# Retention followed by a two-layer MLP with a sine, on one core: the values' columns side by side in PSUM, stores in two pieces, seven products from block 1 on

## The chip, the cores and the metric

The kernel runs on one core of a Trainium2 chip. A core has TensorE (PE; its weight loads are listed as PEld), VectorE (DVE), ScalarE (ACT), GpSimd (POOL) and SyncE (SP), which here issues DMAs; all but SyncE compute. The metric is the device time of one execution in microseconds, median of several runs; lower is better.

## The reference

Eight batches with eight heads, 576 positions and head dimension 64 go through retention (attention without softmax, with a decay), and the result, 4608 rows of 512, through two matrices with h + sin²(alpha h)/alpha between them.

```python
scores = 1/sqrt(64) * np.matmul(q, k.transpose(0, 1, 3, 2))     # q, k, v: (8, 8, 576, 64)
gamma = 1.0 - 2.0 ** (-5.0 - np.arange(8))
Dmat = np.where(rel >= 0, gamma[:, None, None] ** rel, 0.0)      # rel = pos[:, None] - pos
x = np.matmul(scores * Dmat, v)       # then heads side by side: (4608, 512)
h = x @ w_in                          # (512, 2048)
s = np.sin(alpha * h)
g = h + s * s / (alpha + 1e-09)
out = g @ w_out                       # (2048, 512)
```

## The kernel before

**Blocks.** The first 512 positions of each batch are a block, 0 to 7; the last 64 positions of all eight batches form block 8. In a block, positions are taken in chunks of 128 rows: inside a chunk scores are computed and masked, and what came before enters through a state per head.

**One block, step by step.** LD loads 256 positions of q, k or v; partition i holds the two rows 2i and 2i + 1 of a chunk side by side. (k and v of blocks 5 to 7 are loaded with the chunk's two halves of 64 rows instead; `HALVED = 5`.) CA casts to f16 and multiplies in the decay. TU turns q and k on PE, and TK evicts that (blocks 0 and 1); later blocks use a DMA transpose, XP. OU multiplies k and v into the chunks' sums, EV or TS evicts them, and MA, MB and ST make the states from them. SC are the scores, MK the mask. VA and VB multiply masked scores with v: VA for the products whose rows and bank belong to different halves of PE's rows, VB for those of the same half, and between them stands RL, an empty instruction that waits for VA. SA adds the state's part into the same PSUM columns. KP evicts the result to x. Then, for each of 16 units of w_in, PR is the product with w_in, SI the sine, SQ its square and PD the sum g.

**Where the values' columns stand.** VA, VB and SA write 128 columns for a chunk, two groups of 64: rows 2i (r = 0) and rows 2i + 1 (r = 1). The group r goes to every second column, in the rows' own order (lines 574 and 607).

**The product with w_out.** Blocks 0 and 1 do it in the plain way: G2, four units of w_out at a time, for each of four chunks, evicted by FI and stored by OS. From block 2 on it is done with seven products of quarters in place of eight (Strassen in Winograd's form): TT makes differences of w_out's quarters once, SM four sums of g's quarters for each block, each in two pieces, PP the seven products of 8 units and two chunks each, CP copies four of them out of PSUM, AD adds three more, and OQ stores a quarter of the block's output. SM, CP and AD can be given to different engines.

**What sets the order.** The whole program is a list of steps, `STEPS`, written out by a planner. A step's name holds its kind and indices; after a colon stands its engine (A, V, G for ACT, DVE, POOL), and `name=number` places a buffer. Each engine runs its own steps in the list's order and waits by semaphores for what a step reads and writes. All stores and all loads of q, k, v, as well as the DMA transposes, go through SyncE's queue in that order; the loads of w_in (WI, four column groups of 512, units 4g to 4g + 3) and w_out (WO) go through GpSimd's. KB steps are dummy products of zeros on PE (128x256) that keep it at work while it has nothing else in the first blocks.

**Stores.** A partition holds one row of a chunk, so an OS or OQ of blocks 0 to 7 is one DMA of 128 partitions. Block 8's two pieces are two DMAs of 64 partitions, since its rows come from two batches.

Of the kernel before, what the change touches and what calls it, by code (L numbers as in the profile page):

```python
# [23 lines left out]
CN; AR; EY; MC; Z0; ZE; FS; LD.0.q.0 raw.0.q.0=0; LD.0.k.0 raw.0.k.0=1; KB.25.256.6; LE.0.q rs.0.q=0  # L24
LD.0.q.1 raw.0.q.1=2; CA.0.q.0.0:V q16.0.0=1; TU.0.q.0.0 tr.0.q.0=0; LD.0.k.1 raw.0.k.1=3; AT al=1; KB.28.256.6
CA.0.k.0.0:V k16.0.0=2; CA.0.k.0.1:G; LD.0.v.0 raw.0.v.0=4; CA.0.q.0.1:G; CA.0.q.1.2:V q16.0.1=3; WI.2
LD.0.v.1 raw.0.v.1=5; TU.0.q.0.1; TU.0.k.0.0 tr.0.k.0=2; TU.0.k.0.1; KB.2.256.6; TK.0.k.0.0:A kT.0.0=4; TK.0.k.0.1:V
TU.0.q.1.2 tr.0.q.1=3; CA.0.k.1.2:G k16.0.1=5; TK.0.q.0.2:V qT.0.0=6; KB.4.256.2; SC.0.0.0 sc.0.0.0=4
SC.0.0.1 sc.0.0.1=6; KB.4.256.2; MK.0.0.0 ret.0.0.0=7; LD.1.q.1 raw.1.q.1=6; TU.0.k.1.2 tr.0.k.1=0
CA.0.v.0.2:G v16.0.0=8; KB.6.256.2; MK.0.0.1 ret.0.0.1=9; TK.0.k.1.2:A kT.0.1=10; OU.0.0 kv.0.0.0=2 kv.0.0.1=4  # L30
TK.0.q.1.2:V qT.0.1=11; VA.0.0 o.0.0=6; TS.0.0:A kvs.0=7; KB.2.256.0; TS.0.1:V; ST.0.0:G s16.0=12; SC.0.1.1 sc.0.1.1=2
RL.0.0:V; SC.0.1.0 sc.0.1.0=4; WI.0; SA.0.0; VB.0.0; MK.0.1.0 ret.0.1.0=13; KB.21.256.0; LD.1.q.0 raw.1.q.0=8
MA.0.1:G s32.0.1=14; MK.0.1.1 ret.0.1.1=15; MB.0.1:G; CA.0.v.1.2:A v16.0.1=16; WI.1; LD.1.k.0 raw.1.k.0=9
KP.0.0.0:V x.0=10; OU.0.1 kv.0.1.0=0 kv.0.1.1=2; MA.0.2:G s32.0.2=17; VA.0.1 o.0.1=4; TS.0.2:A; KB.3.256.3; ST.0.1:G
RL.0.1:A; KP.0.0.1:A; MB.0.2:V; VB.0.1; KB.7.256.3; ST.0.2:V; MA.0.3:G s32.0.3=18; TS.0.3:V; SA.0.1; AC:V
PR.0.9.0 hps.0.9=0; CA.1.q.1.2:G q16.1.1=19; MB.0.3:V; KP.0.1.0:A; PR.0.8.0 hps.0.8=1; KP.0.1.1:A; KB.2.256.7
PR.0.8.1; LD.1.v.0 raw.1.v.0=11; PR.0.11.2 hps.0.11=2; WI.3; TU.1.q.1.2 tr.1.q.1=3; WO.0; PR.0.1.2 hps.0.1=4
PR.0.3.2 hps.0.3=5; SI.0.1 s.0.1=0; CA.1.q.0.2:V q16.1.0=20; PR.0.2.0 hps.0.2=6; SQ.0.1:G ss.0.1=1; SI.0.3 s.0.3=2
PR.0.9.1; PR.0.2.1; SQ.0.3:A ss.0.3=3; AI; TU.1.q.0.2 tr.1.q.0=7; SI.0.8 s.0.8=4; TK.1.q.1.2:V qT.1.1=21
SI.0.2 s.0.2=5; PD.0.1 gT.0=0; PR.0.0.2 hps.0.0=3; SI.0.11 s.0.11=6; TK.1.q.0.0:V qT.1.0=22; PD.0.3  # L40
PR.0.7.2 hps.0.7=4; SI.0.0 s.0.0=7; SQ.0.11:G ss.0.11=8; TK.1.q.0.1:V; SI.0.9 s.0.9=9; PR.0.6.2 hps.0.6=5
SQ.0.0:V ss.0.0=10; LD.1.k.1 raw.1.k.1=12; SQ.0.2:V ss.0.2=11; PR.0.4.2 hps.0.4=7; SI.0.6 s.0.6=12; PD.0.2
SI.0.7 s.0.7=13; PD.0.11; PR.0.10.2 hps.0.10=6; SQ.0.8:A ss.0.8=14; SQ.0.7:G ss.0.7=15; SQ.0.6:A ss.0.6=2
PR.0.5.2 hps.0.5=2; SQ.0.9:A ss.0.9=0; WO.1; PD.0.7; SI.0.10 s.0.10=1; PD.0.9; CA.1.k.0.2:G k16.1.0=23
PR.0.14.2 hps.0.14=4; SI.0.4 s.0.4=3; PD.0.0; SQ.0.4:A ss.0.4=6; PR.0.13.2 hps.0.13=0; LD.1.v.1 raw.1.v.1=13
SQ.0.10:A ss.0.10=7; PD.0.4; PR.0.12.2 hps.0.12=3; WO.2; LD.2.k.1 raw.2.k.1=14; CA.1.v.0.2:A v16.1.0=24; PD.0.6; WO.3
PR.0.15.0 hps.0.15=7; PD.0.8; SI.0.13 s.0.13=5; G2.0.3.0 op.0.3=5; SI.0.5 s.0.5=11; SQ.0.13:V ss.0.13=8
TU.1.k.0.2 tr.1.k.0=1; SQ.0.5:A ss.0.5=4; PD.0.10; CA.1.k.1.2:G k16.1.1=25; PR.0.15.1; TK.1.k.0.2:A kT.1.0=26; PD.0.5
G2.0.1.0 op.0.1=6; PD.0.13; SI.0.12 s.0.12=12; OU.1.0 kv.1.0.0=1 kv.1.0.1=2; SI.0.14 s.0.14=13; TS.1.1:V kvs.1=15
TS.1.0:V; SQ.0.14:A ss.0.14=9; SC.1.0.1 sc.1.0.1=0; TT.1.1:G T1=1; PD.0.14; TU.1.k.1.2 tr.1.k.1=2; G2.0.3.1  # L50
TK.1.k.1.1:A kT.1.1=27; MK.1.0.1 ret.1.0.1=1; SQ.0.12:A ss.0.12=15; G2.0.0.0 op.0.0=4; TK.1.k.1.0:A; PD.0.12; TT.1.0:G
LD.2.v.1 raw.2.v.1=0; SI.0.15 s.0.15=0; SC.1.0.0 sc.1.0.0=0; SC.1.1.1 sc.1.1.1=2; MK.1.0.0 ret.1.0.0=3
SQ.0.15:A ss.0.15=10; G2.0.1.1; G2.0.3.2; PD.0.15; CA.1.v.1.0:A v16.1.1=4; CA.1.v.1.1:G; MA.1.1:G s32.1.1=2
MK.1.1.1 ret.1.1.1=10; OU.1.1 kv.1.1.0=7 kv.1.1.1=0; TS.1.3:A; SC.1.1.0 sc.1.1.0=0; MB.1.1:V; VA.1.0 o.1.0=2
TT.2.0:V T2=2; G2.0.1.2; MA.1.2:G s32.1.2=6; LD.2.q.0 raw.2.q.0=3; TS.1.2:V; MK.1.1.0 ret.1.1.0=7; G2.0.3.3; MB.1.2:G
# [175 lines left out]
def kernel(  # L231
# [10 lines left out]
    nc = tc.nc  # L242
# [4 lines left out]
    P = 128  # L247
# [686 lines left out]
```

## Time and profile before

| | |
|---|---|
| median of 3 runs | 316.77 us (316.67 to 316.96) |
| profiled execution, and its span | 316.97 us, 315.3 us |
| DMA | 49.88 MB, mean 158 GB/s |
| KB dummies on PE | 104 of 3609 matmuls |

The profile is of one execution. A group of instructions is listed with its line, engine, shapes, count, busy time, mean duration and the idle time ahead of it; the chain of waits is what the end hung on, followed backwards. In a list by time, the first figure is the start in us and the second the time that a merged row takes up. PE's matmuls overlap, so their busy time is larger than the distance from one to the next. A queue (SPq, POOLq) is the part of an engine that issues DMAs.

### The profile page before, as it was taken

What the parts mean: (1) busy time and instruction counts of PE and PEld (TensorE: products, weight loads), DVE (VectorE), ACT (ScalarE), POOL (GpSimd) and SP (SyncE); (2) the same over time, 40 slices, a digit from 0 to 9 for tenths busy, and PEclk for the clock granted to TensorE, in tenths of its full rate; (3) what the DMA queues carried; (4) which work ended last, traced back from release to release, by engine and by line L of the source; (5) the groups of instructions that cost most, each with busy time, mean ns of one, the idle gap of its engine ahead of it and who ended that gap; (6) DMA issues with size and microseconds to landing.
All of it is one profiled execution on the core that took longest, in us unless ns stands there. A gap on an engine that the chain in (4) does not pass through costs nothing.

```text
span 315.3 us, 8643 instructions
## 1 busy us (share of the span) xinstructions
PE 301.4 (96%) x3609; PEld 191.0 (61%) x3609; DVE 247.3 (78%) x354; ACT 184.2 (58%) x295; POOL 200.1 (63%) x174
## 2 busy tenths in 40 slices
PE   8979979999999999999999999999999999999993
PEld 5756444654454555666557657666666567555883
DVE  2656899499997899987778879797799986687732
ACT  1223974484736977858447857666167465678310
POOL 5656576555947857998969689753643534267830
PEclk9999999999999999999999999999999999999999
DMA  8999999459999899838898990626622000110047
GB/s 222 316 281 263 238 233 268 112 120 271 280 238 232 199 184 264 178 78 155 230 241 213 189 202 0 103 52 169 174 85 64 2 0 2 35 67 2 0 136 232
DMA packets 118454, 49.88 MB, mean 158 GB/s; under 512 B 69248, under 2 KB 117392, under 8 KB 118416
## 3 DMA queue, kind: packets, MB, share of 16 engines
q1 hardware_dynamic: 113984, 45.10, 58.8%
q0 software_dynamic: 4224, 4.19, 8.0%
q8 instruction: 28, 0.46, 0.6%
q14 instruction: 10, 0.08, 0.1%
q10 hardware_dynamic: 208, 0.04, 0.1%
HBM read 36.74 MB, written 9.44 MB: 146 GB/s over the span
## 4 chain that ended last, share of the span: by engine, by line
PE 71%; DVE 13%; ACT 4%; DMA 3%; issue 3%; SPq 3%; POOL 2%; POOLq 0%; DVEq 0%; ACTq 0%
PE banks L754 26%; PE banks L855 20%; PE banks L790 9%; PE banks L411 4%; PE banks L573 4%; DVE g L777 4%; PE banks L542 2%; DVE h L555 2%; DVE r L838 2%; PE banks L606 2%; DVE s L773 2%; PE banks L498 2%; ACT s L772 2%; SPq L420 1%; ACT s L762 1%
## 5 line engine op out<-in xcount | busy, mean ns | idle before, releaser
L754 PE MATMUL banks<-r,w_in 128*128 128x512 f16 (+1 forms) x608 | 138.6, 368 | 1.7 <-DVE g L777 1.3
L762 ACT ACTIVATE s<-banks,alpha 128x512 f16<-128x512 f32 x144 | 94.7, 686 | 56.3 <-PE banks L754 55.0
L777 DVE SCALAR_TENSOR_TENSOR g<-s,inva,banks 128x512 f16<-128x512 f16 x144 | 102.0, 741 | 19.9 <-ACT s L772 11.2
L754 PEld LDWEIGHTS <-w_in 128*128 128x128 f16 x608 | 57.4, 98 | 54.9 <-issue 4.4
L855 PEld LDWEIGHTS <-g 128*128 128x128 f16 x560 | 53.7, 98 | 14.8 <-issue 0.6
L773 POOL TENSOR_TENSOR s<-s 128x512 f16<-128x512 f16 x29 | 32.0, 1107 | 38.4 <-ACT s L762 38.4
L447 POOL TENSOR_TENSOR h<-r,cn 128x1024 f16<-128x1024 f32 (+1 forms) x24 | 44.4, 1864 | 5.3 <-DMA r<-in_k_dram 2.8
L772 ACT ACTIVATE s<-s 128x512 f16<-128x512 f16 x76 | 46.1, 628 | 1.2
L838 POOL TENSOR_TENSOR r<-g 128x1024 f16<-128x1024 f16 x15 | 32.5, 2171 | 20.2 <-DVE g L838 10.4
L855 PE MATMUL banks<-w_out,g 128*128 128x256 f16 x336 | 44.5, 273 | 0.0
L329 ACT COPY h<-banks 128x512 f32<-128x512 f32 (+2 forms) x30 | 18.4, 612 | 43.9 <-PE banks L855 23.7
L555 DVE TENSOR_TENSOR h<-banks,mask 128x1024 f16<-128x1024 f32 (+1 forms) x32 | 35.4, 1119 | 7.2 <-PE banks L542 6.3
L790 PE MATMUL banks<-w_out,g 128*128 128x512 f16 x128 | 30.5, 380 | 1.3 <-DVE g L777 1.3
L855 PE MATMUL banks<-r,g 128*128 128x256 f16 x224 | 29.7, 273 | 0.0
L773 DVE TENSOR_TENSOR s<-s 128x512 f16<-128x512 f16 x39 | 22.1, 585 | 7.6 <-ACT s L762 7.6
L855 PEld LDWEIGHTS <-r 128*128 128x128 f16 x224 | 21.7, 98 | 8.1 <-POOL r L838 0.8
L329 ACT CAST r<-banks 128x1024 f16<-128x1024 f32 (+1 forms) x22 | 17.5, 821 | 13.5 <-PE banks L606 9.0
L871 DVE TENSOR_TENSOR h<-banks,h 128x512 f32<-128x512 f32 x21 | 14.3, 687 | 8.7 <-PE banks L855 4.6
L790 PEld LDWEIGHTS <-g 128*128 128x128 f16 x128 | 11.7, 98 | 14.9 <-issue 2.3
L447 DVE TENSOR_TENSOR h<-r,cn 128x512 f16<-128x512 f32 (+1 forms) x16 | 15.4, 979 | 5.8 <-DMA r<-in_q_dram 4.6
L523 POOL TENSOR_TENSOR h<-r,cn 128x256 f32<-128x256 f32 x18 | 12.4, 690 | 10.5 <-DVE r L329 3.9
L573 PE MATMUL banks<-h 64*64 64x128 f16 (+1 forms) x512 | 18.5, 296 | 0.3 <-DVE h L555 0.3
(70 smaller groups left out, 300.3 us busy)
## 6 DMA issues: line engine op xcount, KB each, us to landing
r<-in_q_dram SPq DMA_DIRECT2D x16, 512.0 KB, 6.0
out_dram<-h SPq DMA_DIRECT2D x32, 256.0 KB, 2.8
r<-in_k_dram SPq DMA_DIRECT2D x10, 512.0 KB, 10.0
r<-in_v_dram SPq DMA_DIRECT2D x10, 512.0 KB, 6.7
r<-in_v_dram SPq DMA_DIRECT2D x24, 128.0 KB, 3.3
r<-in_k_dram SPq DMA_DIRECT2D x24, 128.0 KB, 3.7
w_in<-in_moe_w_in_dram POOLq DMA_DIRECT2D x4, 512.0 KB, 9.5
w_out<-in_moe_w_out_dram POOLq DMA_DIRECT2D x4, 512.0 KB, 10.8
```

The source lines that it names most:

```text
L329: return eng.copy(d_, s_) if eng is nc.scalar else eng.tensor_copy(d_, s_)
L447: return eng.tensor_tensor(dst[:, a0:a1].rearrange("p a r t d -> p t (a r) d"), t_.rearrange("p (t a) x -> p t a x", t=2)[:, :, a0:a1].rea ...
L555: return nc.vector.tensor_tensor(ret(b, p, y).rearrange("p t (z x) -> p (t z) x", z=2)[:, :, 0:n], bank(f"sc.{b}.{p}.{y}", 2).rearrange("p ...
L573: made.append(matmul(o[halves(e), t, c : c + 128].rearrange("p (i r) -> p r i", r=2)[:, :, i0:64], v16[halves(g), 4 * t + 2 * x + e, r, :] ...
L754: i = matmul(bank(hps)[:, cols], w_in16[:, a, u * P : (u + 1) * P], x_of(n)[:, a, cols], start=starts(hps), stop=(a == KT - 1), skip_group ...
L762: return nc.scalar.activation(small(f"s.{name}")[:, cols], bank(f"hps.{name}")[:, cols], mybir.ActivationFunctionType.Sin, bias=0.0, scale ...
L772: return nc.scalar.activation(ss_t, s_t, mybir.ActivationFunctionType.Square)
L773: return eng.tensor_tensor(ss_t, s_t, s_t, MULT)
L777: return nc.vector.scalar_tensor_tensor(g_of(n)[:, u, cols], small(f"ss.{name}")[:, cols], inva[:, u : u + 1], bank(f"hps.{name}")[:, cols ...
L790: i = matmul(bank(f"op.{n}.{c}"), g_of(n)[:, fk, c * P : (c + 1) * P], w_out16[:, fk, :], start=starts(f"op.{n}.{c}"), stop=True, skip_gro ...
L838: return eng.tensor_tensor(S[s], a, b, op)
L855: i = matmul(ps[:, 256 * c : 256 * c + 256], left[:, 0, 128 * c : 128 * c + 128], right[:, 0, :], start=starts(f"{BANK_OF[p]}.{n}"), stop= ...
```

## The change

It has four parts.

1. VA, VB and SA write the group r to 64 columns side by side: the first 64 of a chunk's 128 columns hold rows 2i, the next 64 rows 2i + 1. Everything after that has its rows in this order.
2. So a partition p of an output chunk holds row 2i + r with p = 64 r + i. OS and OQ store 64 partitions at a time, each to every second row; OQ does so for all blocks. Stores are now 72 DMAs where there were 40.
3. Block 1 uses the seven products as well: its G2, FI and OS steps (16, 4, 4) go, and 28 PP, 8 SM, 4 CP, 3 AD and 4 OQ come. Only block 0 is left with the plain product.
4. The list of steps is in a new order, with engines and buffers chosen anew: of the KB dummies 65 are left; the differences of w_out's quarters are all made while blocks 0 and 1 run.

```diff
 def values(b, p, same):
-    o[halves(e), t, c : c + 128].rearrange("p (i r) -> p r i", r=2)[:, :, i0:64],
+    o[halves(e), t, c : c + 128].rearrange("p (r i) -> p r i", r=2)[:, :, i0:64],
...
 def SA(b, p):
-    o[halves(e), t, c : c + 128].rearrange("p (i r) -> p r i", r=2),
+    o[halves(e), t, c : c + 128].rearrange("p (r i) -> p r i", r=2),
...
 def rows_of(n, c, m=1):
     if n == 8:
-        return out.rearrange("(b s) d -> b s d", s=S)[2 * c : 2 * c + 2 * m, 512:576, :]
-    return out[576 * n + 128 * c : 576 * n + 128 * (c + m), :]
+        return out.rearrange("(b s) d -> b s d", s=S)[2 * c : 2 * c + 2 * m, 512:576, :].rearrange(
+            "(c r) s d -> r s c d", r=2
+        )
+    r0 = 576 * n + 128 * c
+    return out[r0 : r0 + 128 * m, :].rearrange("(c i r) d -> r i c d", r=2, i=64)
...
 def OS(n, c):
-    x = rows_of(n, c)
-    return nc.sync.dma_start(x.rearrange("b s d -> (b s) d") if n == 8 else x, mid32(f"osb.{n}.{c}"))
+    nc.sync.dma_start(rows_of(n, c)[0, :, 0], mid32(f"osb.{n}.{c}")[halves(0)])
+    return nc.sync.dma_start(rows_of(n, c)[1, :, 0], mid32(f"osb.{n}.{c}")[halves(1)])
...
 def OQ(n, c):
-    if n < 8:
-        return nc.sync.dma_start(x.rearrange("(c p) d -> p c d", p=P), t)
-    x = x.rearrange("(c r) s d -> r s c d", r=2)
     nc.sync.dma_start(x[0], t[halves(0)])
     return nc.sync.dma_start(x[1], t[halves(1)])
...
-CN; AR; EY; MC; Z0; ZE; FS; LD.0.q.0 raw.0.q.0=0; LD.0.k.0 raw.0.k.0=1; KB.25.256.6; LE.0.q rs.0.q=0
+CN; AR; EY; MC; Z0; ZE; FS; LD.0.k.0 raw.0.k.0=0; LD.0.q.0 raw.0.q.0=1; KB.18.256.3; LD.0.q.1 raw.0.q.1=2
```

The order on VectorE from its first step with data, before (L447 casts and decays q and k, L329 evicts, L555 is the mask, L526 and L529 are state steps):

```order
L447 TENSOR_TENSOR h_68<-r_67,cn 128x2x4x64 x2
L447 TENSOR_TENSOR h_68<-r_67,cn 128x2x8x64
L329 COPY h_68<-banks 128x512
L329 COPY h_68<-banks 128x1024
L555 TENSOR_TENSOR h_68<-banks,mask 128x1024 x2
L329 COPY h_68<-banks 128x1024
L329 COPY r_67<-banks 128x256
L555 TENSOR_TENSOR h_68<-banks,mask 128x1024 x2
L329 CAST r_67<-banks 128x2x256
```

The same place after (every line number is 2 higher; L525 and L528 are the state steps MA and MB):

```order
L449 TENSOR_TENSOR h_68<-r_67,cn 128x2x4x64 x2
L331 COPY h_68<-banks 128x1024
L331 COPY h_68<-banks 128x512
L449 TENSOR_TENSOR h_68<-r_67,cn 128x2x8x64
L557 TENSOR_TENSOR h_68<-banks,mask 128x1024 x2
L525 TENSOR_TENSOR h_68<-r_67,cn 128x256
L557 TENSOR_TENSOR h_68<-banks,mask 128x1024
L528 TENSOR_TENSOR r_67<-h_68,r_67 128x256
L557 TENSOR_TENSOR h_68<-banks,mask 128x1024
```

The evictions of turned q and k stand ahead of the second cast, which is k's now, and two state steps came between the mask products; two evictions (of turned q and of a sum) went to ScalarE.

GpSimd at the start, before, from its first step with data (L394 and L397 issue the loads of w_in and w_out):

```order
L447 TENSOR_TENSOR h_68<-r_67,cn 128x2x4x64 x2
L394 DMA w_in_64<-in_moe_w_in_dram 128x4x512
L447 TENSOR_TENSOR h_68<-r_67,cn 128x2x8x64
L329 CAST h_68<-r_67 128x1024
L529 TENSOR_TENSOR h_68<-r_67,cn 128x256
L394 DMA w_in_64<-in_moe_w_in_dram 128x4x512
L523 TENSOR_TENSOR h_68<-r_67,cn 128x256
L526 TENSOR_TENSOR r_67<-h_68,r_67 128x256
L394 DMA w_in_64<-in_moe_w_in_dram 128x4x512
```

The same place after:

```order
L449 TENSOR_TENSOR h_68<-r_67,cn 128x2x4x64 x2
L449 TENSOR_TENSOR h_68<-r_67,cn 128x2x8x64
L396 DMA w_in_64<-in_moe_w_in_dram 128x4x512
L449 TENSOR_TENSOR h_68<-r_67,cn 128x2x8x64
L396 DMA w_in_64<-in_moe_w_in_dram 128x4x512
L531 TENSOR_TENSOR h_68<-r_67,cn 128x256
L396 DMA w_in_64<-in_moe_w_in_dram 128x4x512
```

The first load of w_in moved behind a full cast, and the second and third stand behind fewer steps.

SyncE's queue at its end, before (L655 are DMA transposes of block 8, L877 whole stores, L879 and L880 block 8's pairs):

```order
L655 DMA_TRANSPOSE s_69<-s_69 128x4x128
L877 DMA out_dram<-h_68 128x2x256 x4
L879 DMA out_dram<-h_68 64x2x256
L880 DMA out_dram<-h_68 64x2x256
L877 DMA out_dram<-h_68 128x2x256 x7
L879 DMA out_dram<-h_68 64x2x256
L880 DMA out_dram<-h_68 64x2x256
L879 DMA out_dram<-h_68 64x2x256
L880 DMA out_dram<-h_68 64x2x256
L879 DMA out_dram<-h_68 64x2x256
L880 DMA out_dram<-h_68 64x2x256
```

After, the last loads (L636, of block 8) and the first stores behind them; 17 more such pairs follow to the end:

```order
L657 DMA_TRANSPOSE s_69<-s_69 128x4x128 x2
L881 DMA out_dram<-h_68 64x2x256
L882 DMA out_dram<-h_68 64x2x256
L881 DMA out_dram<-h_68 64x2x256
L882 DMA out_dram<-h_68 64x2x256
L636 DMA h_68<-in_v_dram 64x8x64
L881 DMA out_dram<-h_68 64x2x256
L882 DMA out_dram<-h_68 64x2x256
L881 DMA out_dram<-h_68 64x2x256
L882 DMA out_dram<-h_68 64x2x256
```

Fifteen stores with 19 DMAs stood behind the last transpose; now 19 stores with 38 DMAs stand behind the last load.

More of the change, by code (lines that the diff above doesn't have):

```diff
@@ L29 @@
[L29 to L43, printed above, removed]
@@ L224 @@
[L224 to L226 removed]
+CN; AR; EY; MC; Z0; ZE; FS; LD.0.k.0 raw.0.k.0=0; LD.0.q.0 raw.0.q.0=1; KB.18.256.3; LD.0.q.1 raw.0.q.1=2
+LD.0.k.1 raw.0.k.1=3; CA.0.k.0.1:V k16.0.0=0; TU.0.k.0.1 tr.0.k.0=0; KB.3.256.3; LD.0.v.0 raw.0.v.0=4
+CA.0.q.0.1:V q16.0.0=1; AT al=1; CA.0.q.0.0:G; KB.4.256.3; LE.2.k rs.1.k=2; TU.0.q.0.1 tr.0.q.0=2; KB.4.256.3
@@ new lines @@
+SI.0.14 s.0.14=11; PD.0.5; PR.0.12.2 hps.0.12=1; SI.0.10 s.0.10=12; LD.2.v.0 raw.2.v.0=15; PD.0.13
+SQ.0.14:A ss.0.14=13; G2.0.3.0 op.0.3=2; WO.2; PD.0.7; SQ.0.15:A ss.0.15=14; TU.1.k.0.2 tr.1.k.0=6
+LD.2.k.1 raw.2.k.1=1; SI.0.12 s.0.12=15; PD.0.14; SQ.0.10:G ss.0.10=3; G2.0.3.1; TK.1.k.0.2:A kT.1.0=24; PD.0.15
+CA.1.k.1.2:G k16.1.1=25; G2.0.0.0 op.0.0=3; PD.0.10; LD.2.k.0 raw.2.k.0=0; CA.1.v.1.0:A v16.1.1=26
+SC.1.0.0 sc.1.0.0=6; G2.0.0.1; CA.1.v.1.1:A; MK.1.0.0 ret.1.0.0=27; WO.3; OU.1.0 kv.1.0.0=4 kv.1.0.1=5
@@ L227 @@
+PP.8.3.2; OQ.7.12; CP.7.4:V c21.7=19; PP.8.3.0; PP.8.3.1; OQ.7.21; PP.8.4.1; AD.8.12; PP.8.4.3; PP.8.4.2; OQ.8.12
+PP.8.4.0; CP.8.4:A c21.8=3; OQ.8.21
 """
```

382 lines of the change are left out of this document (195 added, 187 removed).

## The prediction

> **What bounds the kernel now.** I read the page first (span, busy time, chain), then TensorE's groups by shape, then its instructions in order of time, to learn what one step costs.
>
> ```profile
> span 315.3 us, 8643 instructions
> PE 301.4 (96%) x3609; PEld 191.0 (61%) x3609; DVE 247.3 (78%) x354; ACT 184.2 (58%) x295; POOL 200.1 (63%) x174
> PE 71%; DVE 13%; ACT 4%; DMA 3%; issue 3%; SPq 3%; POOL 2%; POOLq 0%; DVEq 0%; ACTq 0%
> ...
> L573 PE MATMUL banks<-h 64*64 64x128 f16 x416 | 18.0, 305 | 0.3 <-DVE h L555 0.3
> L542 PE MATMUL banks<-h 64*64 64x128 f16 x416 | 11.3, 222 | 1.7 <-DVE r L329 0.7 <-ACT r L329 0.5 <-DVE h L555 0.5
> L606 PE MATMUL banks<-h 64*64 64x128 f16 x192 | 8.7, 305 | 1.5 <-issue 1.5
> L498 PE MATMUL banks<-h 64*64 64x64 f16 x512 | 6.3, 196 | 0.1
> ```
>
> TensorE (PE) is busy for 96% of the span and has 71% of the chain: it is the bound nearly everywhere, so what shortens its own stream shortens the kernel, as long as the others keep up. One thing in the groups stands out. The values (L573) and the scores (L542) are the same shape 416 times, 64x64 weights and 128 columns, yet the values take 18.0 us and the scores 11.3. The scores are written side by side into PSUM; the values and the state's part (L606) go to every second column. L498 accumulates as the values do, but side by side, and is quick, so accumulating is not the reason.
>
> The busy time holds modelled ends. The cost of a step is the distance from its start to the next one's:
>
> ```profile
> 100.81 0.42 PE L542 MATMUL banks<-h 64*64 64x128 f16 x16
> 101.16 1.04 PE L790 MATMUL banks<-w_out,g 128*128 128x512 f16 x4
> ...
> 105.58 0.63 PE L573 MATMUL banks<-h 64*64 64x128 f16 x16
> 106.15 1.04 PE L754 MATMUL banks<-r,w_in 128*128 128x512 f16 x4
> ...
> 168.50 0.52 PE L573 MATMUL banks<-h 64*64 64x128 f16 x16
> 168.95 0.60 PE L754 MATMUL banks<-r,w_in 128*128 128x512 f16 x2
> ...
> 222.03 0.37 PE L542 MATMUL banks<-h 64*64 64x128 f16 x16
> 222.33 0.50 PE L855 MATMUL banks<-r,g 128*128 128x256 f16 x3
> ```
>
> A step of 16 score matmuls takes 0.35 us (100.81 to 101.16), one of 16 values 0.57. In blocks 5 to 7, where half of the matmuls have 64 columns, it is 0.30 against 0.45.
>
> **The change, part by part.**
>
> *Columns side by side.* VA and VB run 20 times in blocks 0 to 4 (5 blocks, 2 halves, 2 steps): 20 x (0.57 - 0.35) = 4.4 us. In blocks 5 to 7, 12 x (0.45 - 0.30) = 1.8. SA has 192 matmuls of the slow kind; at the 0.22 us per 16 of the full values that is 2.6. Together **-8.8 us**, all on PE. Bounds: nothing, if the columns are not the cause; 12 us by the busy times (18.0/416 = 43 ns, 8.7/192 = 45, against 11.3/416 = 27). I take the step distances, since they leave out the modelled ends. The evictions to x read the same number of elements as before.
>
> *Seven products in block 1.* 64 matmuls of 512 columns become 112 of 256:
>
> ```profile
> 99.16 0.86 PE banks L790 x4
> 128.92 0.87 PE banks L855 x8
> ...
> L871 DVE TENSOR_TENSOR h<-banks,h 128x512 f32<-128x512 f32 x21 | 14.3, 687 | 8.7 <-PE banks L855 4.6 <-ACT h L329 3.9
> L838 POOL TENSOR_TENSOR r<-g 128x1024 f16<-128x1024 f16 x15 | 32.5, 2171 | 20.2 <-DVE g L838 10.4 <-DVE g L777 9.1 <-PE banks L573 0.7
> L838 DVE TENSOR_TENSOR r<-g 128x1024 f16<-128x1024 f16 x13 | 13.8, 1065 | 0.0
> L329 DVE COPY h<-banks 128x512 f32<-128x512 f32 x11 | 7.5, 684 | 3.5 <-DMA out_dram<-h 2.3 <-PE banks L855 1.1
> ```
>
> 16 groups of 0.86 are 13.8 us, 14 of 0.87 are 12.2: **-1.6 us** on PE. It adds three additions (0.69 us each, on VectorE) and eight sums of quarters; in the new order 36 sums are VectorE's instead of 31 and 28 GpSimd's instead of 25. That is 3 x 0.69 + 5 x 1.07 = 7.4 us more on VectorE and 6.5 on GpSimd. Eleven of VectorE's copies out of PSUM (5 of products, 5 of sums, one last result) move to ScalarE: -7.5. What else moves (wider casts, state products, three more differences of w_out) I put between 0 and +6. VectorE ends up 0 to 6 us busier.
>
> *The start.* The chain of the first 26 us and the rows beside it:
>
> ```profile
> 1.29 5.51 PE banks L411 x25
> 7.39 3.16 PE banks L411 x28
> 17.63 1.52 issue
> ...
> 4.86 0.69 DVE L447 TENSOR_TENSOR h<-r,cn 128x512 f16<-128x512 f32 x1 [3.63 <-DMA r<-in_q_dram]
> 6.80 0.69 DVE L447 TENSOR_TENSOR h<-r,cn 128x512 f16<-128x512 f32 x1 [1.25 <-DMA r<-in_k_dram]
> 6.94 2.45 POOL L447 TENSOR_TENSOR h<-r,cn 128x512 f16<-128x512 f32 x2 [2.84 <-DMA r<-in_k_dram]
> 9.34 0.94 POOL L394 DMA_DIRECT2D w_in<-in_moe_w_in_dram  x1
> 10.31 1.93 POOL L447 TENSOR_TENSOR h<-r,cn 128x1024 f16<-128x1024 f32 x1
> 17.47 2.35 DVE L555 TENSOR_TENSOR h<-banks,mask 128x1024 f16<-128x1024 f32 x2 [0.70 <-PE banks L542]
> 19.82 2.46 PE L411 MATMUL banks<-zero 128*128 128x256 f16 x21
> 25.55 1.05 PE L754 MATMUL banks<-r,w_in 128*128 128x256 f16 x8
> ...
> w_in<-in_moe_w_in_dram POOLq DMA_DIRECT2D x4, 512.0 KB, 9.5
> ```
>
> Block 0's last mask product ends at 19.82, and PE then runs 21 dummies of 2.46 us before it goes on; the first product with w_in starts at 25.55. In the new order no such run stands there (65 dummies in all instead of 104). Followed by the same durations: the first two loads land at 4.86 and 6.80, VectorE multiplies half of k, then half of q, evicts, multiplies k's second part (full width, some 1.5 us) until about 11.5, and does four mask products of 1.2 us with two small state steps of 0.4 among them: 11.5 + 4.8 + 0.9 + gaps is about 18. The last state, values and state products take some 2.5 us: the first product could start near 20.7. Its weights: the first w_in load was issued at 9.34 and now comes after three casts, 6.80 + 2.45 + 1.93 = 11.2; with 9.5 us to land, 20.7 as well. That is 4.9 us earlier than 25.55, of which 0.7 is the faster values of block 0, counted already. Bounds: -4.2, and 0 if the later weights (each quarter is needed in turn) hold the products back. I take **-4.0**, near the row-by-row end, because the other weight issues, too, now stand behind fewer small steps of GpSimd than before.
>
> *Other waits, and two stores for one.*
>
> ```profile
> 96.80:244.60 147.80, 145.96 (x1810) 92.18 (x1809) 126.96 (x180) 98.79 (x156) 106.30 (x85) 1.00 0.70 157
> ...
> 147.81 0.66 SPq L479
> 148.51 0.59 SPq L801
> 151.88 2.96 DMA out_dram<-h
> ...
> 302.21 5.94 SPq L877 DMA_DIRECT2D out_dram<-h  x7
> 311.26 0.59 SPq L879 DMA_DIRECT2D out_dram<-h  x1
> 311.91 0.60 SPq L880 DMA_DIRECT2D out_dram<-h  x1
> ```
>
> The first row is blocks 2 to 6's stage: PE 145.96 of 147.80 us, VectorE (third figure) 126.96, 86%. With some 5 us of PE's work gone there and up to 4 more on VectorE, it reaches 93% of PE's time, so its lateness will show in PE somewhat more often; PE's idle was 1.8 us here. I put **+2.0** (bounds 0 and +8, the latter worked out below). Stores: 40 issues become 72, at 0.6 us on SyncE's queue (0.59 and 0.60; close to 0.65 with the gap to the next): 32 x 0.65 = 21 us of queue. The order puts 19 of the 36 pairs behind the last load, where only PE's last products are waited for; at the very end they are back to back: ten pairs need 13 us while PE has some 10 us left, and a last pair comes after PE's end in both kernels (here at 311.26). I take **+1.0** for that end (0 to +1.5), and nothing for the rest, which the queue's waiting covers: a store waits there for its addition anyway.
>
> [...]
>
> Sum against the profiled execution: 316.97 - 8.8 - 1.6 - 4.0 + 2.0 + 1.0 = 305.6 us. That execution is 0.2 above the median of 316.77, so **305.4**.
>
> **The rivals.**
>
> *VectorE becomes the bound* (0.15). If it can't be busier than the 86% of that stage, 127 + 4 us of work need 152 there, against the 145 that I forecast: +8, near 313. For it: VectorE's 13% of the chain. Against it: nearly all of its idle time is waiting for ScalarE and PE, which come earlier now.
>
> *The columns aren't the cause* (0.04): 305.4 + 8.8 = 314.2. Scores and state products read their moving columns alike and differ in the output alone, which speaks against it.
>
> *The stores' issue lands on the path* (0.05): the transposes and loads of blocks 4 to 7 queue behind stores on SyncE, as from 147.81 on, where the chain runs through a transpose and a store on the queue to a store's landing at 154.84. With all 21 us on the path it is 326; from 11.4 us on it is slower than before. Against: most of the new pairs come after the loads.
>
> *The clock* (0.06). The first 25 dummies take 220 ns each, the next 28 only 113: PE starts at half pace. If the fewer dummies leave gaps that bring this back, block 0's attention (some 6.5 us of PE) takes up to 3 us more: 308.4. The longest idle of PE in the first 26 us was 1.5 us, and the pace held. [...]
>
> **How the numbers follow.** The forecast has 0.70, with its own range 302 to 308: down by 3.2 us if the extra waits are none and the columns give a little more, up by 2.6 if the start gives only half. The range 302 to 311 takes in the clock and half of VectorE's case. A change of 0.2% is about what a measurement of this kernel can tell: over it faster in all cases but the stores' and the worst of VectorE's, 0.92; slower 0.05; within 0.03.
>
> **What would show it.** Values and scores of one shape with equal distances (0.35 us); PE's sum of busy time near 287 (301.4 - 8.8 - 1.6, and 39 dummies less at 0.11); the first product with w_in near 21 us; PE idle in blocks 2 to 6 below 5 us; the last store's issue within 3 us of PE's end. I am wrong if PE waits for VectorE's sums or for transposes by more than 8 us in all, or if the first product with w_in stays after 24 us.

## The result, and the profile after

The changed kernel takes 314.91 us (median of 5 runs, 313.37 to 319.86); its ratio to the kernel before is 0.9921, 95% interval 0.9898 to 0.9943. It is faster, by 0.8%, where 3.6% were forecast, and it lies 3.9 us above the range. Its profiled execution took 319.86 us at a granted clock of 0.978 where most executions have 0.99 or more, so times by stage are read from near-twins at full clock below, and all medians here count such executions while the ratios leave them out. The page after:

```profile
span 318.2 us, 8713 instructions
...
PE 292.2 (92%) x3618; PEld 186.6 (59%) x3618; DVE 251.8 (79%) x355; ACT 193.7 (61%) x315; POOL 189.5 (60%) x164
...
PEclk9999999999799999999997979999999999999997
...
PE 57%; DMA 17%; DVE 7%; ACT 5%; issue 4%; POOL 4%; SPq 4%; POOLq 0%; ACTq 0%; DVEq 0%
```

TensorE did less (292.2 us, 301.4 before) in a longer span. Its share of the chain fell from 71% to 57%, and transfers rose from 3% to 17%: the work went down, and the waiting went up. (With whole stores, in `new_whole` below, transfers have 12% of the chain and TensorE 65%, so most of that rise does not come from the pairs.) TensorE's 64x64 groups by shape:

```profile
L544 PE MATMUL banks<-h 64*64 64x128 f16 x416 | 12.0, 226 | 0.8 <-ACT h L331 0.6 <-DVE h L557 0.2
L575 PE MATMUL banks<-h 64*64 64x128 f16 x416 | 11.7, 220 | 0.5 <-DVE h L557 0.3 <-DVE h L876 0.2
...
L608 PE MATMUL banks<-h 64*64 64x128 f16 x192 | 5.5, 221 | 0.9 <-POOL h L531 0.6 <-POOLq L589 0.2
```

The values (L575) now cost what the scores (L544) do: 11.7 us instead of 18.0, and the state's part 5.5 instead of 8.7. TensorE in order of time, at the first product with w_in and at one step of values, and the last 22 stores on SyncE's queue (first and last):

```profile
20.00 0.61 PE L756 MATMUL banks<-r,w_in 128*128 128x256 f16 x4 [0.46 <-DMA w_in<-in_moe_w_in_dram]
...
104.32 0.42 PE L575 MATMUL banks<-h 64*64 64x128 f16 x16
104.67 0.61 PE L860 MATMUL banks<-w_out,g 128*128 128x256 f16 x4
```

```profile
299.76 0.60 SPq L881 DMA_DIRECT2D out_dram<-h  x1
...
314.76 0.61 SPq L882 DMA_DIRECT2D out_dram<-h  x1
```

The first product starts at 20.00 us, held for the last 0.46 by its weights. A step of values takes 0.35 us. At the end 22 stores stand back to back: the last is issued at 314.76, and TensorE ended at 311.2, so 7.0 us of the span stand behind its last product (4.8 before).

### The profile page after: what moved, and what is told of

It reads as the page before. It is cut to its first block, busy times and chain, and to the rows that moved or that the text cites. A ratio compares the mean times of both kernels' runs of the same rounds, so it can differ in the third digit from the quotient of the medians.

```text
span 318.2 us, 8713 instructions
## 1 busy us (share of the span) xinstructions
PE 292.2 (92%) x3618; PEld 186.6 (59%) x3618; DVE 251.8 (79%) x355; ACT 193.7 (61%) x315; POOL 189.5 (60%) x164
## 2 busy tenths in 40 slices
DMA packets 119479, 49.89 MB, mean 157 GB/s; under 512 B 69760, under 2 KB 118928, under 8 KB 119440
## 4 chain that ended last, share of the span: by engine, by line
PE 57%; DMA 17%; DVE 7%; ACT 5%; issue 4%; POOL 4%; SPq 4%; POOLq 0%; ACTq 0%; DVEq 0%
PE banks L756 26%; PE banks L860 24%; DMA w_out<-in_moe_w_out_dram 5%; DMA r<-in_q_dram 5%; DMA r<-in_v_dram 4%; ACT h L331 2%; PE banks L795 2%; ACT s L764 2%; SPq L422 2%; DVE h L449 2%; DMA r<-in_k_dram 2%; PE banks L544 2%; POOL r L843 1%; DMA h<-h 1%; POOL h L449 1%
## 5 line engine op out<-in xcount | busy, mean ns | idle before, releaser
L860 PEld LDWEIGHTS <-g 128*128 128x128 f16 x640 | 61.2, 98 | 18.9 <-issue 1.9
L860 PE MATMUL banks<-w_out,g 128*128 128x256 f16 x384 | 50.9, 274 | 0.1
L331 ACT COPY h<-banks 128x512 f32<-128x512 f32 (+2 forms) x38 | 23.2, 619 | 35.5 <-PE banks L860 23.5
L860 PE MATMUL banks<-r,g 128*128 128x256 f16 x256 | 35.0, 273 | 1.0 <-ACT h L331 1.0
L331 ACT CAST r<-banks 128x512 f16<-128x512 f32 (+1 forms) x21 | 15.9, 795 | 16.7 <-PE banks L608 9.9
L449 DVE TENSOR_TENSOR h<-r,cn 128x1024 f16<-128x1024 f32 (+1 forms) x14 | 18.5, 1329 | 6.7 <-DMA r<-in_k_dram 3.5
L331 ACT CAST h<-r 128x1024 f16<-128x1024 f32 (+1 forms) x16 | 14.5, 917 | 4.9 <-DMA r<-in_v_dram 4.6
L795 PE MATMUL banks<-w_out,g 128*128 128x512 f16 x64 | 16.0, 380 | 1.3 <-issue 0.9
L860 PE MATMUL banks<-w_out,r 128*128 128x256 f16 x128 | 17.1, 273 | 0.0
L531 POOL TENSOR_TENSOR h<-r,cn 128x256 f16<-128x256 f32 x18 | 13.0, 725 | 6.8 <-DVE r L528 4.9
```

Of the source, the lines that this page charges most:

```text
L331: return eng.copy(d_, s_) if eng is nc.scalar else eng.tensor_copy(d_, s_)
L449: return eng.tensor_tensor(dst[:, a0:a1].rearrange("p a r t d -> p t (a r) d"), t_.rearrange("p (t a) x -> p t a x", t=2)[:, :, a0:a1].rea ...
L795: i = matmul(bank(f"op.{n}.{c}"), g_of(n)[:, fk, c * P : (c + 1) * P], w_out16[:, fk, :], start=starts(f"op.{n}.{c}"), stop=True, skip_gro ...
L860: i = matmul(ps[:, 256 * c : 256 * c + 256], left[:, 0, 128 * c : 128 * c + 128], right[:, 0, :], start=starts(f"{BANK_OF[p]}.{n}"), stop= ...
```

## The experiments

Every run is timed beside the kernel before on the same chip (316.85 to 317.27 us); ratios are to it, with 95% intervals. "Whole" stores are one DMA of 128 partitions per output piece, as before the change; block 8's four pieces stay two DMAs of 64 partitions in all kernels. Some kernels serve only to take the time apart: with columns side by side and no pairs to every second row (`old_columns`, `new_whole`, `new_plain1`, and those with two or three pieces or adjacent rows) rows end up in another place within their chunk, and `half_only` never writes half of the rows of blocks 0 to 7. Lines of `STEPS` are shown cut short.

### The change taken apart

`old_columns` is the kernel before with part 1 alone; `old_columns_pairs` adds part 2, the pairs of stores, as in the change's diff.

```diff
-    o[halves(e), t, c : c + 128].rearrange("p (i r) -> p r i", r=2)[:, :, i0:64],
+    o[halves(e), t, c : c + 128].rearrange("p (r i) -> p r i", r=2)[:, :, i0:64],
...
-    o[halves(e), t, c : c + 128].rearrange("p (i r) -> p r i", r=2),
+    o[halves(e), t, c : c + 128].rearrange("p (r i) -> p r i", r=2),
```

> The kernel before with the columns side by side and nothing else; a store stays one DMA, so rows stand in another place within their chunk of 128. If PE's stream is the bound, as predicted, 16 matmuls of values step by 0.35 us in place of 0.57 and the end comes 6 to 9 us earlier (308 to 311 us). If what PE saves turns into waits in any order written for the slower columns, less than 3 us.

> The same with two stores of 64 rows a piece, as in the change, in the old order. If the queue's 32 further issues are covered, within 1 us of the kernel with the columns alone; if they delay loads and transposes, 3 us and more slower than that.

The columns alone: 310.9 us, 0.9803 (0.9762 to 0.9845), a gain of 6.0. With the pairs: 322.5 us, 1.019 (1.0159 to 1.022). In the old order the pairs cost 11.6 us and turn the gain into a loss. In the profiled execution with the pairs 9.2 us stand behind TensorE's last product (4.8 before), and TensorE ran at half clock twice on the way, for 3.41 us from 20.2 and from 228.4 (granted clock 0.99 over the 311.4 us up to its last product; see the last section).

`new_whole` is the changed kernel with whole stores; `new_spread_whole` has spread columns besides, so that order and block 1 remain of the change.

```diff
-    nc.sync.dma_start(rows_of(n, c)[0, :, 0], mid32(f"osb.{n}.{c}")[halves(0)])
-    return nc.sync.dma_start(rows_of(n, c)[1, :, 0], mid32(f"osb.{n}.{c}")[halves(1)])
+    x = rows_of(n, c)
+    return nc.sync.dma_start(x.rearrange("b s d -> (b s) d") if n == 8 else x, mid32(f"osb.{n}.{c}"))
...
+    if n < 8:
+        return nc.sync.dma_start(x.rearrange("(c p) d -> p c d", p=P), t)
```

> The changed kernel with whole stores of 128 rows (rows stand in another place within their chunk). If the doubled stores eat the gain: 5 to 8 us faster than the changed kernel (307 to 310). If only its last few us hang on them: 1.5 to 3 us faster (311.5 to 313.5), and the waits for loads in the middle stay.

> The changed order with the columns spread as before and whole stores: the new order and block 1's seven products alone. If the order itself is what loses, this is slower than the kernel before by some 3 us or more (above 319); if the order is as good as the old one and only the columns fall short, it is at 313 to 316.

`new_whole`: 307.58 us, 0.9728 (0.9684 to 0.9772). In the new order the pairs cost 7.3 us by the medians (314.91 less 307.58), 6.1 by the ratios. `new_spread_whole`: 310.83 us, 0.9816 (0.9793 to 0.9838). So order and block 1 bring 6.0 us, a better time than in either of the two cases expected, and the columns in that order only 3.3.

Why only 3.3, though the step of values is faster? TensorE's own part is there: its busy time is 294.8 us with spread columns and 287.3 side by side. But the stretch of block 1's products, with spread columns first, then side by side, shows where some of it goes (length of the stretch, then busy time of PE, PEld, DVE, ACT, POOL, granted clock, DMA share, GB/s):

```profile
51.50:85.10 33.60, 32.45 (x497) 19.43 (x490) 30.14 (x37) 24.97 (x43) 23.08 (x21) 1.00 0.89 208
```

```profile
50.60:84.10 33.50, 30.58 (x496) 17.95 (x489) 30.18 (x37) 24.97 (x43) 23.36 (x21) 1.00 0.92 208
```

TensorE is busy 1.9 us less and the stretch is as long: here the saving became waiting. A second place is in block 4, where TensorE stops in the middle of a step of scores and no engine is shown to release it: for 0.76 us in `new_spread_whole` and for 1.60 in `new_whole`. From the first step of values ahead of that wait to its end it is 3.79 us with spread columns (173.33 to 177.12) and 3.71 side by side (171.67 to 175.38).

`new_plain1` has whole stores and does block 1 in the plain way, in the places of the steps that it replaces; two differences of w_out's quarters (TT) are made later for it.

```diff
...
-PP.1.1.3 X.1=3; SQ.1.14:A ss.1.14=3; PP.1.1.2
+G2.1.0.0 op.1.0=3; SQ.1.14:A ss.1.14=3; G2.1.0.1
...
```

> The changed order and columns with whole stores (rows stand in another place within their chunk), but block 1 by the plain product: 64 matmuls of 512 columns at places of the 112 of 256, no sums for it, the in-place difference of w_out made after it. If the seven products bring what their columns say (13.8 against 12.2 us on PE), this is 1 to 2 us slower than with them (308.5 to 310). If the sums and additions they need eat that, it is as fast or faster (306 to 307.6).

307.46 us, 0.9632 (0.9577 to 0.9687), against 307.58 and 0.9728 for `new_whole`: the medians are alike, and the intervals of the ratios touch. The seven products in block 1 bring nothing that can be measured.

### What in the pairs costs

The candidates were the number of issues, pieces of 64 partitions, rows that are written two apart, and the time that issues hold SyncE's queue. `new_two_whole` stores two pieces of 128 partitions with half of the columns each; `new_pairs_adjacent` two pieces of 64 partitions to 64 adjacent rows each.

```diff
+    nc.sync.dma_start(x[:, 0:256], t[:, 0:256])            # new_two_whole, in OS
+    return nc.sync.dma_start(x[:, 256:512], t[:, 256:512])
...
+    nc.sync.dma_start(x[0:64], t[halves(0)])               # new_pairs_adjacent, in OS
+    return nc.sync.dma_start(x[64:128], t[halves(1)])
```

> The changed order and columns with 72 stores as in the change, but each piece has all 128 partitions and half of the columns (one chunk of two, or half of the 512 columns); rows stand in another place within their chunk. If the cost of the pairs is the queue's time for 32 more issues (0.65 us each), it is as slow as the changed kernel: 313 to 316 us. If it is the shape, 64 partitions a piece, it is as fast as with whole stores, 307 to 309.

> The changed order and columns with every store as two pieces of 64 partitions, as in the change, but to 64 adjacent rows in place of every second row (rows stand in another place within their chunk). If the cost lies in the piece of 64 partitions (0.61 us to issue, against 0.33 to 0.46 for 128), it is as slow as the changed kernel, 313 to 316 us; if it lies in writing every second row, it is as fast as with pieces of 128 partitions, 307 to 310.

308.83 us, 0.9755 (0.9705 to 0.9806), and 314.17 us, 0.9898 (0.9847 to 0.9949). As many issues cost 1.2 us in the one shape and 6.6 in the other, and rows two apart are not the reason. That looked like the shape. But a piece of 64 partitions also takes longer to issue, which the same line shows, first in the changed kernel, then in `new_two_whole` (duration min/median/max in ns, first and last start):

```profile
L882 SPq DMA_DIRECT2D out_dram<-h x32: 605/610/1667, 102.2 to 314.8; - x32
```

```profile
L882 SPq DMA_DIRECT2D out_dram<-h x28: 332/460/1679, 98.1 to 298.4; - x28
```

Two more runs told the two apart. `new_three_whole` stores three pieces of 128 partitions; `half_only` leaves out one store of each pair.

```diff
+    nc.sync.dma_start(x[:, 0:128], t[:, 0:128])            # new_three_whole, in OS
+    nc.sync.dma_start(x[:, 128:256], t[:, 128:256])
+    return nc.sync.dma_start(x[:, 256:512], t[:, 256:512])
...
-    nc.sync.dma_start(rows_of(n, c)[0, :, 0], mid32(f"osb.{n}.{c}")[halves(0)])    # half_only
```

> The new order, columns side by side, and every output piece stored as three DMAs of 128 partitions each (a quarter, a quarter and a half of its 512 columns; rows elsewhere in their chunk, as in the other kernels with stores of 128 partitions). Block 8's last four pieces stay two DMAs of 64 partitions, so 104 issues in place of 72. At some 0.45 us an issue the stores take about 50 us of SyncE's queue, as much as the pairs of 64 partitions do (49.6 us), and two such pieces took 41. Theory A, the queue's time: what the pairs cost is the time that their issues hold the queue, whatever their shape, so this comes out like the pairs, 313 to 315 us. Theory B, the shape: what costs is that a piece spans 64 partitions, by something besides the time of its issue, so this stays with the two pieces of 128 partitions, 308 to 310 us.

> The changed kernel with the first of the two stores of each pair left out, except for block 8's last four pieces: half of the output's rows are never written. The remaining 40 or so issues are of 64 partitions, at 0.61 us each, so the stores take some 24 us of SyncE's queue, as with whole stores (24.7 us), and half the bytes. Theory A, the queue's time: the price of the pairs is gone, 307 to 309 us. Theory B, the shape: part of the price stays with the pieces of 64 partitions that are left, 310 us or more.

316.37 us, 0.9967 (0.9941 to 0.9994), and 308.89 us, 0.9759 (0.9725 to 0.9793). All kernels of the new order with columns side by side, by the sum of the durations of their stores' issues in the profiled execution:

| stores | issues | us of queue | median us | ratio |
|---|---|---|---|---|
| whole | 40 | 24.7 | 307.58 | 0.9728 |
| one half of each pair | 40 | 28.6 | 308.89 | 0.9759 |
| 2 x 128 partitions | 72 | 41.2 | 308.83 | 0.9755 |
| 2 x 64, adjacent rows | 72 | 49.5 | 314.17 | 0.9898 |
| 2 x 64, every second row (the change) | 72 | 49.6 | 314.91 | 0.9921 |
| 3 x 128 partitions | 104 | 55.1 | 316.37 | 0.9967 |

Over these six kernels the time rises with the queue's time and not with the shape: pieces of 128 partitions cost as much as pieces of 64 once they hold the queue as long, and pieces of 64 are cheap while there are few. The number of issues does not order them (72 cost 1.2 us or 7.3), nor do the packets that the pages count (119,479 with adjacent rows, 119,991 with two pieces of 128). Two points are less clean than the others: `half_only` also moves half of the bytes, and `new_three_whole`, which came out above the 313 to 315 us expected, has 124,600 packets. It is no straight line: the first 16.5 us of queue cost about 1, which the intervals hardly tell from nothing, the next 8.4 cost 6.

Where do they cost? One execution of each by stretches, block 4's products and the tail after TensorE's last, for `new_whole`, then `new_pairs_adjacent`, then `new_three_whole`:

```profile
146.40:177.70 31.30, 28.86 (x383) 18.57 (x382) 29.41 (x42) 18.87 (x30) 26.16 (x19) 1.00 0.80 186
...
301.40:306.10 4.70, 0.01 (x1) 0.00 (x0) 0.00 (x0) 0.59 (x1) 0.00 (x0) 0.83 0.47 112
```

```profile
145.70:179.80 34.10, 29.21 (x383) 18.59 (x380) 31.50 (x42) 18.84 (x30) 25.89 (x19) 1.00 0.69 170
...
304.10:311.20 7.10, 0.01 (x1) 0.00 (x0) 0.00 (x0) 0.59 (x1) 0.00 (x0) 0.86 0.65 156
```

```profile
146.70:180.10 33.40, 30.18 (x383) 18.80 (x380) 30.07 (x42) 18.83 (x30) 27.49 (x20) 0.95 0.70 178
...
304.50:312.40 7.90, 0.00 (x0) 0.00 (x0) 0.00 (x0) 0.58 (x1) 0.00 (x0) 0.80 0.56 151
```

Block 4 takes 2.8 and 2.1 us longer, the tail 2.4 and 3.2. The tail is plain: finished stores are still being issued when TensorE ends. In block 4 TensorE waits at two places. One is a wait in the middle of a step of scores (L544), with whole stores and then with pairs:

```profile
175.38 0.22 PE L544 MATMUL banks<-h 64*64 64x64 f16 x2 [1.60 <-issue]
```

```profile
177.51 0.22 PE L544 MATMUL banks<-h 64*64 64x64 f16 x3 [2.35 <-issue]
```

1.60 us against 2.35. It is the wait that has 0.76 us with spread columns; it is taken up under the hardware below. The other wait is there with pairs only. VectorE's state steps and GpSimd's squares, first in `new_whole` (no wait of TensorE follows), then in `new_pairs_adjacent`:

```profile
164.87 0.41 DVE L528 TENSOR_TENSOR r<-h,r 128x256 f32<-128x256 f32 x1
165.21 0.41 DVE L531 TENSOR_TENSOR h<-r,cn 128x256 f16<-128x256 f32 x1
...
165.29 2.23 POOL L775 TENSOR_TENSOR s<-s 128x512 f16<-128x512 f16 x2 [2.06 <-ACT s L764]
```

```profile
165.00 1.25 DVE L528 TENSOR_TENSOR r<-h,r 128x256 f32<-128x256 f32 x1
166.18 1.25 DVE L531 TENSOR_TENSOR h<-r,cn 128x256 f16<-128x256 f32 x1
...
164.84 2.31 POOL L775 TENSOR_TENSOR s<-s 128x512 f16<-128x512 f16 x2 [1.49 <-ACT s L764]
...
168.14 1.89 PE L756 MATMUL banks<-r,w_in 128*128 128x512 f16 x8 [1.34 <-DVE g L779]
```

With whole stores VectorE's steps begin first and take 0.41 us each; with pairs they begin 0.16 us after GpSimd's and take 1.25 each, the next sum of g is late, and TensorE waits 1.34 us. `new_three_whole` has no such wait; there TensorE loses the rest at half clock (0.95 in its row). So the table ties the price to the queue's time, and the tail is shown to be one of its places. How it reaches block 4 differs from one execution to the next, by shifts of tenths of a microsecond, and no run isolates it; that it does so through these two waits is read from single executions.

### Moving the late stores and loads

In the changed kernel's own execution VectorE waited in its order for a load that had been issued late, and TensorE behind it:

```profile
163.17 2.78 DVE L449 TENSOR_TENSOR h<-r,cn 128x1024 f16<-128x1024 f32 x1 [2.36 <-DMA r<-in_q_dram]
...
166.66 3.65 PE L756 MATMUL banks<-r,w_in 128*128 128x512 f16 x10 [3.60 <-DVE g L779]
```

At the end, OQ.7.22 waited for its sum from 288.9 to 299.8, with finished pieces of blocks 2, 4 and 5 behind it. `pairs_tail` moves those ahead of it; `pairs_loads` moves two loads of q for block 6 forward, the first past three loads of k, the second past one; `pairs_both` does both.

```diff
-PP.8.5.0; OQ.7.22; PP.8.5.2; PP.8.6.0; OQ.4.11; PP.8.6.1;                          # pairs_tail
+PP.8.5.0; OQ.4.11; OQ.5.12; OQ.2.22; OQ.7.22; PP.8.5.2; PP.8.6.0; PP.8.6.1;
...
-SQ.3.13:A ss.3.13=2; LD.6.k.1 raw.6.k.1=0; PD.3.11;                                # pairs_loads
+SQ.3.13:A ss.3.13=2; LD.6.q.0 raw.6.q.0=6; LD.6.k.1 raw.6.k.1=0; PD.3.11;
...
-MK.5.0.1 ret.5.0.1=14; LD.7.k.1 raw.7.k.1=4;
+MK.5.0.1 ret.5.0.1=14; LD.6.q.1 raw.6.q.1=11; LD.7.k.1 raw.7.k.1=4;
```

> The changed kernel with three stores that are ready early (of blocks 4, 5 and 2) moved ahead of the store that waits for block 7's sum at 299.7 us, nothing else. If the end hangs on six issues (3.9 us) too many behind that wait, the last issue follows the last eviction at once: 2 to 2.5 us faster than the changed kernel (312 to 313). If the last stores are held by something else, no difference.

> The changed kernel with two loads of block 6's q moved ahead of loads of block 6's and 7's k in the queue, so they are issued before 152 us in place of 156, nothing else. If VectorE's wait for that load at 160.8 us and PE's stall of 3.6 us behind it come from the queue, that stall and the half clock after it go: 3 to 5 us less in the profile than an execution that has them (319.9), 1 to 3 us in the median. If PE stalls there for something else, it stays.

> The changed kernel with both moves, the three early stores and the two loads of q. If the stores cost it the end and that one stall, the gains add up: 1.9 + 2.6 us off 314.9, 309.5 to 311.5, near the pieces of 128 partitions. If the stall only moves to the next late load, no better than the end's share alone, 312 to 313.

313.01 us, 0.9867 (0.9827 to 0.9908); 312.29 us, 0.9822 (0.9758 to 0.9887); 312.22 us, 0.9823 (0.977 to 0.9876). The first gets back 1.9 us by the medians, the second 2.6, both together 2.7; by the ratios it is 1.7, 3.1 and 3.1. For the first the interval overlaps the changed kernel's, but its trace shows the place: 5.1 us stand behind TensorE's last product, where the changed kernel has 7.0. Both together give no more than one alone; the full sum of the gains would be a ratio of 0.977, at the edge of the interval, so that they do not add up is likely and not shown. In the profiled execution of `pairs_loads` (321.51 us) the wait of 3.60 us is gone and others came, the longest 2.79 us at 223.16. So no single place was found that holds the price.

### Whole stores with the rows in order

The pairs were there because part 1 leaves rows in another order. KP's eviction can put them back: it writes x with every second f16 element, and the pieces go out whole. For that x is laid out as two halves, and a product with w_in reads its columns from both. `new_unpermute` does it in the new order, `old_unpermute` in the old one. Nothing of the computation is left out or moved in them.

```diff
+    def xh_of(n):
+        return big16(f"x.{n}").rearrange("p (h y) -> p h y", h=2)
...
-                x_of(b)[:, :, cols].rearrange("p (t x) n -> p t x n", t=2),
-                bank(f"o.{b}.{p}", 2).rearrange("p t (x n) -> p t x n", x=2),
+                xh_of(b)[:, p].rearrange("p (c i r) -> p c r i", r=2, i=64),
+                bank(f"o.{b}.{p}", 2).rearrange("p t (c r i) -> p (t c) r i", r=2, i=64),
```

> The changed order and columns with whole stores; the eviction from PSUM to x puts the rows back into their own order (it writes every second f16 element), so the output's rows stand where they belong. If that writing costs ScalarE and VectorE nothing, 307 to 308.5 us; at 0.5 us more for each of 20 evictions, most of it beside PE's work, 308.5 to 311. Slower than 313 would say that the eviction is on the path.

> The old order with the columns side by side and whole stores; the eviction to x puts the rows back, so the output's rows stand where they belong. If what the columns save reaches the end in the old order as in the first run (310.9), and the slower eviction (1.31 us a piece in place of 1.01, measured in the new order) is hidden, 310 to 312 us; if the evictions are on the path, 313 to 316.

308.16 us, 0.9716 (0.9665 to 0.9766), and 312.4 us, 0.9839 (0.9783 to 0.9895). The first beats both the kernel before and the changed one. The second lies between the two cases expected, and its interval overlaps that of `old_columns`, so what the eviction costs there is open. ScalarE's share of this eviction, in `new_whole` and then in `new_unpermute`:

```profile
L331 ACT CAST r<-banks 128x1024 f16<-128x1024 f32 x10 | 9.9, 1012 | 12.0 <-PE banks L608 8.2 <-PE banks L575 3.6
```

```profile
L331 ACT CAST r<-banks 128x1024 f16<-128x1024 f32 x10 | 12.8, 1311 | 11.5 <-PE banks L608 7.7 <-PE banks L575 3.6
```

0.3 us more for each of ten, and 4.0 us more of ScalarE in all (197.4 us busy, 193.4 in `new_whole`), on an engine that is busy for 64% of the span, in place of some 7 us for the pairs.

## Why the prediction was wrong, and where it was right

**The step that failed** is "+1.0 for that end (0 to +1.5), and nothing for the rest, which the queue's waiting covers". The pairs cost 7.3 us. The tail's part was too small: 2.4 us and not 1.0, because ready stores stood behind one that waited; moved ahead of it in `pairs_tail`, they took 1.9 us off the tail. And the waiting does not cover the rest. There is much of it, but in a few places; SyncE's queue in the changed kernel (waited for: us in total, times, longest):

```profile
SPq L881 <- DVE h L876: 42.3, 4, 21.8
```

42.3 us of it are four waits, the longest 21.8. Where a store waits 21.8 us a second one of 0.61 can hide, an estimate from these two figures. In block 4, where stores, loads and transposes follow one another closely, it does not: that stretch is 2.8 us longer with the pairs. The rival "the stores' issue lands on the path" names blocks 4 to 7 and had 0.05; part of the price was indeed in block 4. Its size was not right: it took 21 us of queue one for one, while 24.9 us more of queue (49.6 less 24.7) cost 7.3. Its mechanism, a load behind stores, is seen in one execution (2.36 us, above) and, moved, gave back 2.6 us; other waits make up the rest. That most of the new pairs come after the loads was no argument: of the 5.1 us between the spans of `new_pairs_adjacent` and `new_whole` more than half arise in block 4, ahead of the last loads.

The 21 us of queue were not right either. They count the 32 further issues alone, as if a whole store held the queue as long as a half one. That seven whole stores took 5.94 us does not show it: the row spans a gap, and the seven issues took 0.37 to 0.59 us each, where a half takes about 0.6.

The halves as such are not the reason for the price: three pieces of 128 partitions cost as much (316.37 us, and 314.91 with two of 64).

**Columns: right in kind, too large in time.** -8.8 us were forecast. The step went from 0.57 to 0.35 us as read off the scores, and TensorE's busy time fell by 7.5 (294.8 less 287.3), but the kernel won 6.0 in the old order and 3.3 in the new. So this term failed as well, in its step from TensorE to the kernel: the sum took every microsecond of TensorE for one of the kernel, while the two stretches above show the saving become waiting. That the columns were the cause holds: the same 416 matmuls took 18.0 us spread and 11.7 side by side.

**Block 1: -1.6 forecast, nothing measured** (307.58 against 307.46). TensorE's saving was not on the path there.

**The start and the order.** -4.0 and +2.0 were forecast, -3.6 with block 1; measured is -6.0 for all three, 2.4 us more than forecast. That was luck, and it hid part of the miss. The first product came at 20.00 us (20.7 forecast, 25.55 before). The stretch of block 1's products, before and after, one wait of TensorE in it after, and then all up to the end of that stretch, before and in `new_spread_whole`:

```profile
59.80:96.80 37.00, 37.00 (x469) 19.58 (x468) 30.43 (x43) 22.16 (x37) 23.93 (x23) 1.00 0.89 214
```

```profile
50.30:84.60 34.30, 31.63 (x496) 18.69 (x490) 30.38 (x38) 25.06 (x43) 23.90 (x21) 0.96 0.93 211
...
PE banks L500 <- POOL h L449: 2.2, 1, 2.2
```

```profile
0.00:96.80 96.80, 90.14 (x1193) 53.91 (x1194) 72.48 (x102) 49.92 (x81) 61.15 (x69) 1.00 1.00 236
```

```profile
0.00:85.10 85.10, 76.95 (x1115) 46.43 (x1116) 66.87 (x91) 52.86 (x89) 55.24 (x64) 1.00 1.03 235
```

TensorE had no idle time in this stretch before and 2.7 us after, 2.2 of it for one of GpSimd's casts. Still `new_spread_whole`, order and block 1 alone, is 11.7 us ahead at its end, and only 5.6 at the end of the span (309.7 and 315.3). By then it has run 78 matmuls fewer, 39 of them dummies, so part of the lead is work put off; where the rest was lost again was not separated.

**The signs named.** Equal steps of 0.35 us: yes. TensorE's busy time near 287: 287.3 in `new_whole`, 292.2 in the changed kernel's own execution, part of it at half clock (below). TensorE idle in blocks 2 to 6 below 5 us: with pairs it is 4.9 in block 4 alone (34.10 - 29.21). The last store's issue within 3 us of TensorE's end: no, it ends 4.2 later. VectorE did not become the bound: 251.8 us busy, 247.3 before. The clock did not fall at the start, where the rival had put it (1.00 up to 20.00 us in the changed kernel); in the old order with columns side by side it did (`old_columns_pairs` and `old_unpermute`, for 3.41 us from 20.2 and 20.3; granted clock 0.979 and 0.994 over the whole execution). Neither sign of being wrong came: TensorE waited 5.2 us for VectorE's sums in its products with w_in, under the 8 named, and the first product was early. Apart from the last store, none of the signs watched the stores.

Without the stores' term the sum would have been 304.4; `new_whole` measured 307.58. So of the miss of 9.5 us, 6.3 are the stores and 3.2 the rest: the columns fell 5.5 short, and order and block 1 brought 2.4 more than forecast.

## What to carry to other kernels

Cost a store or load at the place in its queue where it stands, by what follows it at once; the queue's waiting in total says nothing about a piece that a load stands behind. When a layout makes stores longer to issue (0.61 us against 0.46 here), look first for an eviction that can undo it: here 4.0 us of an engine with room replaced some 7 us of the kernel. A saving on the engine that is the bound was not worth its full size here (7.5 us of TensorE's busy time, 3.3 of the kernel in the new order), so time each part of a large change by itself.

## What the runs showed of the hardware

Half clock after a wait. TensorE's granted clock (the figure before the last two) in three stretches that each follow a wait: in the changed kernel after 3.60 us, in `new_three_whole` after 2.39, in `new_pairs_adjacent` after 2.35:

```profile
167.49:170.90 3.41, 3.41 (x9) 1.22 (x8) 3.36 (x7) 0.69 (x1) 0.00 (x0) 0.50 0.65 155
```

```profile
177.00:180.40 3.40, 3.40 (x26) 1.18 (x24) 1.79 (x3) 1.12 (x2) 3.40 (x4) 0.62 0.48 107
```

```profile
178.00:181.40 3.40, 3.40 (x34) 1.70 (x32) 2.31 (x4) 2.00 (x3) 3.40 (x3) 1.00 0.49 106
```

The wait of 2.39 us was followed by it (from 176.16 to 179.57 us, so the row holds only part of it) and the one of 2.35 was not. The length of the wait alone does not tell the two kinds apart: in the changed kernel waits of 2.23 us (to 82.33) and 2.29 (to 183.20) go with half clock too, from 82.15 and from 184.55 us, though both are shorter than 2.35. Where the wait was 1.60 us (`new_whole`) or 1.76 (`half_only`), the stretch of block 4 has 1.00. What decides was not shown.

In the changed kernel's execution half clock came three times (the dips in the page's PEclk row, from 82.15, 167.49 and 184.55 us), for 3.41 us each, which costs up to 1.7 us a time, an estimate from half of that length, and is part of why that execution is 5 us above the median. The prediction had put the rival of the clock at the start, behind gaps between the dummies; it came in blocks 1 and 4, behind waits for sums and casts and behind the one that the last paragraph takes up.

A store's issue took longer with 64 partitions than with 128: 0.61 us in the changed kernel against 0.46 in `new_two_whole` (medians of L882, above) for the same 128 KB.

A wait of TensorE that no engine is shown to end. In six kernels of the new order with columns side by side TensorE stops in the middle of the same step of scores (L544), after 12 to 14 of its 16 matmuls: for 1.60 us in `new_whole`, 1.76 in `half_only`, 1.89 in `new_two_whole`, 2.29 in the changed kernel, 2.35 in `new_pairs_adjacent` and 2.39 in `new_three_whole`. With spread columns, in `new_spread_whole`, it is 0.76. What TensorE waits for there was not shown, nor why the wait differs from one kernel to the next.
